# Retention and two MLPs on one core: second MLP in groups of two blocks and two chunks, first layer by seven products

## The chip, the cores and the metric

One Trainium2 chip, one core of it. The metric is the device time of one execution in microseconds (us). The engines are TensorE (PE, its weight loads are listed apart as PEld), VectorE (DVE), ScalarE (ACT), GpSimd (POOL) and SyncE (SP, whose queue SPq issues DMAs).

## What is computed

Linear attention with a decay per head, then an MLP whose activation is h·cos(h), then an MLP with a piecewise activation. There are 4·768 = 3072 tokens, a model width of 512 and a hidden width of 2048.

```python
state = gamma * state + k[t] v[t]^T ;  y[t] = scale * q[t] state      # attention, per head
h = x @ w_in;  g = h * cos(h);  x = g @ w_out                         # first MLP
h = x @ w_in                                                          # second MLP
g = where(h >= 1, h, where(h <= -1, 0, (h + 1)**2 / 4))
out = g @ w_out
```

## The kernel before

Tokens are handled in NB = 6 blocks of TB = 512, the hidden width in NF = 16 chunks of 128, the model width in NP = 4 slices of 128. Every operand of a matmul of the MLPs is kept as two tiles of type fp32r, a high part and a low part (`high_part`, an ACT copy, and `low_part`, a POOL subtraction, L100 to L108), and a product takes three matmuls: high·high, low·high and high·low. Weights arrive as 64-bit numbers and are turned into fp32 on the chip by `Convert` (L115), whose steps `one` to `six` are spread over later steps by `Conveyor` (L173).

The order of the work on each engine is written out by hand: `tc.manual_schedule()` (L637) keeps the program's order on each engine and on each DMA queue, and a tile pool makes an instruction that writes a buffer wait until those that used it have finished. A step (k, b, j) takes block b and chunk j through `first` (L396: 12 matmuls into a PSUM bank), `act` (L408: activation and the split of the result into high and low) and, LAG = 3 steps later, `second` (L463: 12 matmuls that add to four PSUM banks, which `evacuate`, L485, empties at the end of a block).

k = 0 is the first half of the first MLP's chunks, with the attention of the next block beside it, k = 1 the second half, and k = 2 the whole second MLP. During k = 1 the weights of the second MLP are converted: half of them stay in SBUF, half are stored to DRAM and come back in the first block of k = 2. In k = 2 a step is 12 matmuls of `first`, a clamp on DVE (L427), a square on ACT (L436), a maximum on DVE (L454), a copy on ACT (L455), a subtraction on DVE (L458) and 12 matmuls of `second`. The loop over k = 1 and k = 2 is L597 to L630, and L631 to L635 finish the last three steps.

## Time and profile before

| | us |
|---|---|
| median of 3 runs (lowest, highest) | 1182.93 (1182.03, 1183.85) |
| the profiled execution, its own time | 1180.83 |
| its span in the trace | 1179.0 |
| PE busy | 1150.0 (98%) |
| DVE busy | 614.6 (52%) |
| ACT busy | 522.6 (44%) |
| POOL busy | 261.8 (22%) |

The page of the profile lists the engines' busy time, the span in 40 slices, the DMA queues, the chain of work that ended last, the costliest groups of instructions and the DMA issues. A matmul is pipelined: its listed duration of 0.39 us overlaps the next one, so the rate is read from the start of one to the start of the next, or from a window's count of matmuls. DVE and ACT list overlapping durations in the same way when one instruction follows another that it doesn't depend on.

### The profile page before, as it was taken

To read this page: it belongs to the slowest core of one execution; us is meant where nothing else is said; L and a number is where in the kernel's file an instruction comes from. 1 tells how busy PE (TensorE), PEld (TensorE's weight loads), DVE (VectorE), ACT (ScalarE), POOL (GpSimd) and SP (SyncE) were. 2 spreads that over 40 slices of the span, in tenths; PEclk is the share of its full clock that TensorE was granted. 3 is DMA by queue.
4 is the path that set the end of the run, shared out by engine and by line. 5 is a ranking of instruction groups with operands and counts; after the bars stand their busy time and mean duration, and the time that the engine had idled before them with its cause. 6 is when DMAs were issued, how large, how long until landed. Compare 5 with 4: busy or idle time off the path is not lost.

```text
span 1179.0 us, 15370 instructions
## 1 busy us (share of the span) xinstructions
PE 1150.0 (98%) x6026; PEld 942.9 (80%) x6026; DVE 614.6 (52%) x981; ACT 522.6 (44%) x854; POOL 261.8 (22%) x216
## 2 busy tenths in 40 slices
PE   6788999999999999999999999999999999999998
PEld 4567888888888888888888888888888888888887
DVE  5898776565434467667765434333333433434332
ACT  3465554444436666577677423223222223223221
POOL 2665332221104212224437401001001001001000
PEclk7889999999999999999999999999999999999999
DMA  7636476453136447536425300200200200200000
GB/s 275 260 127 250 171 276 225 153 196 117 64 116 232 144 151 256 203 139 232 178 99 196 116 1 1 72 1 1 72 1 1 72 1 1 72 1 1 36 1 36
DMA packets 47848, 133.92 MB, mean 114 GB/s; under 512 B 5408, under 2 KB 5920, under 8 KB 43936
## 3 DMA queue, kind: packets, MB, share of 16 engines
q1 hardware_dynamic: 41440, 111.97, 26.9%
q10 hardware_dynamic: 6336, 20.97, 4.5%
q8 instruction: 47, 0.77, 0.3%
q14 instruction: 25, 0.20, 0.1%
HBM read 93.08 MB, written 39.85 MB: 113 GB/s over the span
## 4 chain that ended last, share of the span: by engine, by line
PE 92%; DVE 4%; DMA 1%; ACT 1%; issue 1%; SPq 0%; POOL 0%; DVEq 0%; ACTq 0%
PE b L479 44%; PE b L402 43%; PE b L284 2%; PE b L336 1%; PE b L342 1%; DVE cs L153 1%; DVE cf L138 1%; DMA raw<-in_w 1%; DMA qk<-in_qk 1%; DVE cf L149 1%; PE b L307 1%; DVE cs L134 0%; DVE pm L296 0%; DVE b L454 0%; ACT gh L455 0%
## 5 line engine op out<-in xcount | busy, mean ns | idle before, releaser
L402 PE MATMUL b<-xh,wih 128*128 128x512 f32 x768 | 302.5, 394 | 14.5 <-DVE pm L296 9.4
L402 PE MATMUL b<-xh,wil 128*128 128x512 f32 x768 | 302.7, 394 | 4.1 <-POOL wil L104 4.1
L427 DVE TENSOR_SCALAR r<-b 128x512 f32<-128x512 f32 x96 | 66.4, 691 | 304.0 <-PE b L402 304.0
L402 PE MATMUL b<-xl,wih 128*128 128x512 f32 x768 | 207.6, 393 | 0.0
L436 ACT ACTIVATE r<-r,half 128x512 f32<-128x512 f32 x96 | 69.4, 723 | 286.2 <-DVE r L427 286.2
L402 PEld LDWEIGHTS b<-xh,wih 128*128 128x128 f32 x768 | 145.8, 190 | 46.2 <-ACT wih L101 13.7
L402 PEld LDWEIGHTS b<-xh,wil 128*128 128x128 f32 x768 | 145.8, 190 | 36.3 <-POOL wil L104 6.0
L402 PEld LDWEIGHTS b<-xl,wih 128*128 128x128 f32 x768 | 146.0, 190 | 30.6
L479 PE MATMUL b<-gh,woh 128*128 128x512 f32 x384 | 153.9, 401 | 0.0
L479 PE MATMUL b<-gh,wol 128*128 128x512 f32 x384 | 149.7, 390 | 0.0
L479 PE MATMUL b<-woh,gh 128*128 128x512 f32 x384 | 149.4, 389 | 0.0
L479 PE MATMUL b<-wol,gh 128*128 128x512 f32 x384 | 149.4, 389 | 0.0
L454 DVE TENSOR_TENSOR b<-b,r 128x512 f32<-128x512 f32 x192 | 133.7, 696 | 29.7 <-ACT r L436 17.8
L159 POOL TENSOR_TENSOR cf<-cf,cs 128x512 f32<-128x512 f32 x64 | 83.0, 1297 | 294.5 <-DVE cs L153 239.6
L421 DVE SCALAR_TENSOR_TENSOR r<-b,r 128x512 f32<-128x512 f32 x96 | 66.2, 689 | 157.7 <-ACT r L416 154.6
L455 ACT ACTIVATE gh<-b 128x512 fp32r<-128x512 f32 x192 | 114.4, 596 | 74.5 <-DVE b L454 74.3
L458 DVE TENSOR_TENSOR gl<-b,gh 128x512 fp32r<-128x512 f32 x192 | 130.7, 681 | 1.8 <-ACT gh L455 0.7
L416 ACT ACTIVATE r<-b 128x512 int32<-128x512 f32 x96 | 56.9, 593 | 152.7 <-PE b L402 152.3
L104 POOL TENSOR_TENSOR xl<-xl,xh 128x512 fp32r<-128x512 f32 x24 | 30.9, 1289 | 390.7 <-ACT xh L101 390.7
L479 PE MATMUL b<-gl,woh 128*128 128x512 f32 x384 | 108.5, 389 | 0.0
L479 PE MATMUL b<-woh,gl 128*128 128x512 f32 x384 | 105.5, 389 | 0.0
L479 PEld LDWEIGHTS b<-gh,woh 128*128 128x128 f32 x384 | 72.0, 188 | 18.1 <-issue 0.7
(55 smaller groups left out, 1284.4 us busy)
## 6 DMA issues: line engine op xcount, KB each, us to landing
raw<-in_w SPq DMA_DIRECT2D x64, 512.0 KB, 5.7
qk<-in_qk SPq DMA_DIRECT2D x23, 512.0 KB, 5.4
w<-cf ACTq DMA_DIRECT2D x32, 256.0 KB, 4.3
v<-in_v SPq DMA_DIRECT2D x24, 256.0 KB, 5.5
xTh<-xh ACTq DMA_DIRECT2D x6, 1024.0 KB, 4.1
xTl<-xl ACTq DMA_DIRECT2D x6, 1024.0 KB, 6.0
yp<-o SPq DMA_DIRECT2D x24, 256.0 KB, 2.8
xh<-xTh SPq DMA_DIRECT2D x6, 1024.0 KB, 6.7
```

The costliest lines, as they stand in the source:

```text
L104: nc.gpsimd.tensor_tensor(out=lo, in0=x, in1=hi.bitcast(F32), op=ALU.subtract)
L159: nc.gpsimd.tensor_tensor(out=self.f, in0=self.f, in1=self.s.bitcast(F32), op=ALU.mult)
L284: nc.tensor.matmul(out=s2[r][:, p, :], lhsT=t[o:o + D, 1, p, :], rhs=t[o:o + D, 0, p, :], start=True, stop=True,)
L402: nc.tensor.matmul(out=h, lhsT=w[:, c * P:(c + 1) * P], rhs=x[:, c, :], start=(i == 0), stop=(i == len(terms) - 1),)
L416: nc.scalar.activation(out=n, in_=h, func=AF.Identity, scale=INV_2PI)
L421: nc.vector.scalar_tensor_tensor(out=r, in0=h, scalar=INV_2PI, in1=n, op0=ALU.mult, op1=ALU.subtract)
L427: nc.vector.tensor_scalar(out=r, in0=h, scalar1=-1.0, scalar2=1.0, op0=ALU.max, op1=ALU.min)
L436: nc.scalar.activation(out=r, in_=r, func=AF.Square, scale=0.5, bias=half)
L454: nc.vector.tensor_tensor(out=self.h, in0=self.h, in1=self.r, op=op)
L455: nc.scalar.activation(out=self.gh, in_=self.h, func=AF.Copy)
L458: nc.vector.tensor_tensor(out=self.gl, in0=self.h, in1=self.gh.bitcast(F32), op=ALU.subtract)
L479: nc.tensor.matmul(out=acc[k, b][e], lhsT=l, rhs=r, start=(begin and i == 0), stop=(last and i == 2),)
```

## The change

k = 2 is gone from the loop over steps; the class `Products` does the second MLP. It takes the six blocks in three pairs (p) and the sixteen chunks in eight pairs (l), which gives 24 groups g of two blocks and two chunks. A group's first layer is a product of 2 by 2 blocks (chunk by model half, times model half by block), done by Strassen's scheme in Winograd's form: seven products (`product`, six matmuls each, named "11", "t2", "t1", "22", "t3", "21", "t4") and sums of them on DVE (`plus`), in place in PSUM where it can be.

The sums of the weights (`combine`, four POOL operations of half width for a group) are made during k = 1 and stored to DRAM; each group loads its weights (`load_w1`, `load_w2`, from SP) and splits them (`split_w1`, `split_w2`: ACT copy, POOL subtraction). The differences of the inputs (`make`: `load`, `sub`, `parts`) are made during k = 1 for the first pair of blocks; for the other two pairs they are made while the pair before runs, up to four of the list's twenty entries at the end of each of its first five groups (`ready[:4]` in `run`), and stored to DRAM (`xb_d`) through a high-part tile `xhi` that has two buffers; `load_x` brings them back.

The clamp and the square become three ACT operations (`square`). The second layer of group g runs as eight `output`s of six matmuls between the products of group g + 1; each ends in one of PSUM banks 0 to 3, and DVE adds it to a sum in SBUF (`add`), which is stored to `out` after the eighth pair of chunks. The products use banks 4 to 7, in the order 4, 5, 6, 7, 4, 5, 4 in one group and 7, 6, 5, 4, 7, 6, 7 in the next. The high and low part of a group's last result (`late`) are made at the start of the next group.

In the loop of k = 1, conversions start in three steps of four, all results go to DRAM, `raw` has two buffers where it had three, and `cf` four where it had three.

```diff
+ORDER = ("11", "t2", "t1", "22", "t3", "21", "t4")
+LEFT = dict(zip(ORDER, ((0, 0), (1, 1), (1, 0), (2, 1), (2, 0), (0, 1), (3, 0))))
...
-        for m in range(2) for j in range(NH, NF) for a in range(2)
+        for m, j, a in [(0, j, a) for j in range(NH, NF) for a in range(2)] + [(1, j, 1) for j in range(NF)]
...
+    wa_d = [[dram.tile([P, n], F32, name=f"wa{g}{i}") for i, n in enumerate((TB, TB, TB, TB // 2))]
+            for g in range(NH)]
...
-            self.raw = self.stage.tile([P, TB, 2], I32, tag="raw", name="raw", bufs=3)
+            self.raw = self.stage.tile([P, TB, 2], I32, tag="raw", name="raw", bufs=3 - self.m)
...
-            ncs = 3 if self.m == 0 else 2
+            ncs, ncf = ((3, 3), (2, 4))[self.m]
...
-            self.f = self.stage.tile([P, TB], F32, tag="cf", name="cf", bufs=3)
+            self.f = self.stage.tile([P, TB], F32, tag="cf", name="cf", bufs=ncf)
...
+            elif (self.m, self.a) == (1, 0):
+                combine(self.j, self.f)
...
+    def combine(j, f):
+        left[j % 2] = f
+        if j % 2 == 0:
+            return
+        g, h = j // 2, TB // 2
+        a11, a12, a21, a22 = [left[i][:, o:o + h] for i in range(2) for o in (0, h)]
+        s12, s34 = [stage1[0].tile([P, TB], F32, tag=t, name=t) for t in ("s12", "s34")]
+        s1, s2, s3, s4 = [t[:, o:o + h] for t in (s12, s34) for o in (0, h)]
+        for o, x, y, op in (
+            (s1, a21, a22, ALU.add), (s3, a11, a21, ALU.subtract),
+            (s2, s1, a11, ALU.subtract), (s4, a12, s2, ALU.subtract),
+        ):
+            nc.gpsimd.tensor_tensor(out=o, in0=x, in1=y, op=op)
+        for d, t in zip(wa_d[g], (left[0], s12, s34, a22)):
+            nc.scalar.dma_start(out=d, in_=t)
...
+    class Products:
...
+        def load_w1(self, g):
+            self.w1[g] = [self.pool1("wi", NH + NP * (g % 2) + n) for n in range(NP)]
+            for d, (_, lo) in zip(wa_d[g % NH], self.w1[g]):
+                nc.sync.dma_start(out=lo[:, :d.shape[1]].bitcast(F32), in_=d)
+        def split_w1(self, g, a, b):
+            for d, (hi, lo) in list(zip(wa_d[g % NH], self.w1[g]))[a:b]:
+                split(hi[:, :d.shape[1]], lo[:, :d.shape[1]])
+        def load_w2(self, g):
+            self.w2[g] = [self.pool1("wo", NH + 2 * (g % 2) + i) for i in range(2)]
+            for i, (_, lo) in enumerate(self.w2[g]):
+                nc.sync.dma_start(out=lo.bitcast(F32), in_=w32_d[1, 2 * (g % NH) + i, 1])
+        def split_w2(self, g):
+            for w in self.w2[g]:
+                split(*w)
...
+        def make(self, p, c):
+            at, x = {}, {}
+            def load():
+                if p == 0:
+                    at.update({q: self.pool0(2 * n + c) for n, q in enumerate(ORDER)})
+                    for q in ORDER:
+                        self.x[0, q, c] = at[q]
+                    x.update({q: at[q][1].bitcast(F32) for q in ("11", "21", "22")})
+                    x["12"] = at["t4"][0].bitcast(F32)
...
+                else:
+                    for q in ORDER + ("12",):
+                        x[q] = self.tmp.tile([P, TB], F32, tag=f"x{q}", name=f"x{q}")
+                for q, j, e in (("11", 0, c), ("12", 1, c), ("21", 0, c + 2), ("22", 1, c + 2)):
+                    nc.sync.dma_start(out=x[q], in_=yT_d[2 * p + j][:, e, :])
+            def sub(o, a, b):
+                nc.gpsimd.tensor_tensor(out=x[o], in0=x[a], in1=x[b], op=ALU.subtract)
+            def parts(q):
+                if p == 0:
+                    hi, lo = at[q]
+                else:
+                    hi = self.tmp.tile([P, TB], F32R, tag="xhi", name="xhi", bufs=2)
+                    lo = x[q].bitcast(F32R)
+                high_part(hi, x[q])
+                low_part(hi, lo, x[q])
+                if p:
+                    for d, t in zip(xb_d[p, q, c], (hi, lo)):
+                        nc.sync.dma_start(out=d, in_=t.bitcast(F32))
...
+            return [
+                load,
+                some(lambda: sub("t1", "12", "11"), lambda: sub("t3", "22", "12")),
+                some(lambda: sub("t2", "22", "t1"), lambda: sub("t4", "21", "t2")),
+            ] + [lambda q=q: parts(q) for q in ORDER]
+        def load_x(self, p, n):
+            if p >= NB // 2:
+                return
+            q, c = ORDER[n // 2], n % 2
+            t = self.x[p, q, c] = self.spare.pop(0)
+            for o, d in zip(t, xb_d[p, q, c]):
+                nc.sync.dma_start(out=o.bitcast(F32), in_=d)
...
+        def product(self, g, q, i):
+            tile, half = LEFT[q]
+            p, to = g // NH, bank(i)
+            wh, wl = self.w1[g][tile]
+            xs = [self.x[p, q, c] for c in range(2)]
+            terms = [(c, w, x[0]) for c, x in enumerate(xs) for w in (wh, wl)]
+            terms += [(c, wh, x[1]) for c, x in enumerate(xs)]
+            for n, (c, w, x) in enumerate(terms):
+                o = half * 2 * P + c * P
+                nc.tensor.matmul(
+                    out=to, lhsT=w[:, o:o + P], rhs=x, start=n == 0, stop=n == len(terms) - 1
+                )
+            if g % NH == NH - 1:
+                self.free_x(p, q)
+                n = 2 * ORDER.index(q)
+                for m in range(NP + n, min(NP + n + 2, 14)):
+                    self.load_x(p + 1, m)
+            return to
+        def square(self, g, i, n, h):
+            r = tp.tile([P, TB], F32, tag="r", name="r", bufs=5)
+            nc.scalar.activation(out=r, in_=h, func=AF.Relu, scale=-0.5, bias=half)
+            nc.scalar.activation(out=r, in_=r, func=AF.Relu, scale=-1.0, bias=one)
+            nc.scalar.activation(out=r, in_=r, func=AF.Square)
+            self.g[g, i, n] = h, r
+        def high(self, g, i, n):
+            h, r = self.g[g, i, n]
+            m = self.ng % 8
+            self.ng += 1
...
-                nc.sync.dma_start(out=out[t0:t0 + P, :], in_=o)
+                gh, gl = self.pool1("wo", NF - 8 + m)
+            nc.vector.tensor_tensor(out=h, in0=h, in1=r, op=ALU.max)
+            nc.scalar.activation(out=gh, in_=h, func=AF.Copy)
+            self.g[g, i, n] = h, gh, gl
+        def low(self, g, i, n):
+            h, gh, gl = self.g[g, i, n]
+            nc.vector.tensor_tensor(out=gl, in0=h, in1=gh.bitcast(F32), op=ALU.subtract)
+            self.g[g, i, n] = gh, gl
+        def output(self, g, n, e):
+            y = bank(self.nl % 4)
+            self.nl += 1
+            s = slice(e * P, (e + 1) * P)
+            for i in range(2):
+                gh, gl = self.g[g, i, n]
+                wh, wl = self.w2[g][i]
+                for m, (a, w) in enumerate(((gh, wh), (gh, wl), (gl, wh))):
+                    nc.tensor.matmul(
+                        out=y, lhsT=a[:, s], rhs=w, start=(i, m) == (0, 0), stop=(i, m) == (1, 2)
+                    )
+            self.out.append((g, n, e, y))
+        def add(self):
+            if not self.out:
+                return
+            g, n, e, y = self.out.pop(0)
+            a = self.acc[n][:, e, :]
+            if g % NH == 0:
+                nc.vector.tensor_copy(out=a, in_=y)
+            else:
+                nc.vector.tensor_tensor(out=a, in0=y, in1=a, op=ALU.add)
+            if g % NH == NH - 1:
+                t0 = (e * NC + 2 * (g // NH) + n) * C
+                nc.sync.dma_start(out=out[t0:t0 + P, :], in_=a)
...
+        def group(self, g, outs, late):
+            more = g + 1 < self.NG
+            a, b, c, d = (4, 5, 6, 7) if g % 2 == 0 else (7, 6, 5, 4)
...
+            p1 = self.product(g, "11", a)
+            self.add()
+            for f in late[:1]:
+                f()
+            s1 = self.sums(0)
+            nc.scalar.activation(out=s1, in_=p1, func=AF.Copy)
+            for f in late[1:]:
+                f()
+            outputs(1)
+            p6 = self.product(g, "t2", b)
+            if more:
+                self.split_w1(g + 1, 0, 3)
+            self.add()
+            u = plus(self.sums(1), p6, s1)
+            outputs(1)
+            p5 = self.product(g, "t1", c)
+            self.add()
+            s5 = self.sums(2)
+            nc.scalar.activation(out=s5, in_=p5, func=AF.Copy)
+            outputs(1)
+            if more:
+                self.split_w1(g + 1, 3, NP)
+            self.split_w2(g)
+            h12 = self.product(g, "22", d)
+            self.add()
+            plus(h12, h12, u)
+            plus(h12, h12, s5)
+            self.square(g, 0, 1, h12)
+            outputs(1)
+            p7 = self.product(g, "t3", a)
+            self.add()
+            u2 = plus(self.sums(3), p7, u)
+            h22 = plus(p5, p5, u2)
+            self.high(g, 0, 1)
+            self.square(g, 1, 1, h22)
+            outputs(1)
+            self.low(g, 0, 1)
+            h11 = self.product(g, "21", b)
+            self.add()
+            plus(h11, h11, s1)
+            self.high(g, 1, 1)
+            self.square(g, 0, 0, h11)
+            outputs(1)
+            self.low(g, 1, 1)
+            h21 = self.product(g, "t4", a)
+            if g + 2 < self.NG:
+                self.load_w1(g + 2)
+            self.add()
+            plus(h21, h21, u2)
+            self.high(g, 0, 0)
+            self.square(g, 1, 0, h21)
+            outputs(1)
+            self.low(g, 0, 0)
+            self.add()
+            outputs(1)
+            if more:
+                self.load_w2(g + 1)
+            return [lambda: self.high(g, 1, 0), lambda: self.low(g, 1, 0)]
+        def run(self, before):
+            self.NG = NB // 2 * NH
+            self.tmp = sbuf("tmp", 1)
+            t = [xpool.tile([P, NP, TB], F32R, tag=t, name=t) for t in ("xh", "xl")]
+            self.spare = [[a[:, c, :] for a in t] for c in range(NP)]
+            self.load_w1(1)
+            self.load_w2(0)
+            last = parts.pop()
+            late = [last.high, last.low]
...
+            for g in range(self.NG):
+                if g == 0:
+                    outs = iter([f for b in before for f in (b, lambda: None)])
+                else:
+                    outs = iter([
+                        lambda g=g, n=n, e=e: self.output(g - 1, n, e) for n in (1, 0) for e in range(NP)
+                    ])
+                p, l = divmod(g, NH)
+                if l == 0 and p + 1 < NB // 2:
+                    ready = self.right_sides(p + 1)
+                if l == NH - 2:
+                    for n in range(NP):
+                        self.load_x(p + 1, n)
+                late = self.group(g, outs, late)
+                if g == 0:
+                    t = [xpool.tile([P, NP, TB], F32R, tag=t, name=t) for t in ("xh", "xl")]
+                    self.acc = [a.bitcast(F32) for a in t]
+                for f in ready[:4]:
+                    f()
+                ready = ready[4:]
+            for f in late:
+                f()
+            for n in (1, 0):
+                for e in range(NP):
+                    self.output(self.NG - 1, n, e)
+                    self.add()
+            while self.out:
+                self.add()
...
+            todo = [
+                Convert(1, j + i, a, False) for j in range(0, NF, 2) for a in range(2) for i in range(2)
+            ]
...
+                conv.start(todo.pop(0) if todo and k == 1 and l % 4 != 3 else None, stage)
...
+                if (k, b, l) == (1, 2, LAG + 1):
+                    ready = fast.right_sides(0)
+                if ready:
+                    fill.append(ready.pop(0))
...
+                if (k, b, l) == (1, NB - 1, NP + 1):
+                    fast.load_w1(0)
+                if (k, b, l) == (1, NB - 1, NH - 1):
+                    fast.split_w1(0, 0, NP)
...
+        fast.run([lambda i=i: evacuate(iter(second(i)), NP) for i in range(i - LAG, i)])
...
```

## Rows read from the trace of the kernel before

**Rows 1.** The page's busy time, share of the span and instructions.

```profile
PE 1150.0 (98%) x6026; PEld 942.9 (80%) x6026; DVE 614.6 (52%) x981; ACT 522.6 (44%) x854; POOL 261.8 (22%) x216
```

**Rows 2.** Windows by stage: busy (instructions) per engine, granted clock, DMA share, GB/s.

```profile
500.00:600.00 100.00, 100.00 (x442) 82.78 (x442) 70.30 (x117) 70.28 (x118) 38.46 (x29) 1.00 0.48 174
653.02:1175.21 522.19, 522.19 (x2304) 432.06 (x2302) 198.13 (x300) 145.96 (x229) 35.94 (x28) 1.00 0.07 25
```

**Rows 3.** The chain that ended last: start, length, what.

```profile
1161.62 2.72 PE b L402 x12
1164.34 10.89 PE b L479 x48
```

**Rows 4.** Groups by form, 620 to 1179 us: busy and mean ns, idle before.

```profile
L454 DVE TENSOR_TENSOR b<-b,r 128x512 f32<-128x512 f32 x102 | 71.3, 699 | 21.1 <-ACT r L436 17.8 <-ACT r L434 3.3
L427 DVE TENSOR_SCALAR r<-b 128x512 f32<-128x512 f32 x96 | 66.4, 691 | 304.0 <-PE b L402 304.0
L104 POOL TENSOR_TENSOR xl<-xl,xh 128x512 fp32r<-128x512 f32 x24 | 30.9, 1289 | 390.7 <-ACT xh L101 390.7
```

**Rows 5.** Timeline of one step, 723 to 726 us: start, length, engine, line.

```profile
723.74 0.69 DVE L427 TENSOR_SCALAR r<-b 128x512 f32<-128x512 f32 x1 [3.26 <-PE b L402]
724.34 0.68 DVE L458 TENSOR_TENSOR gl<-b,gh 128x512 fp32r<-128x512 f32 x1
724.46 0.72 ACT L436 ACTIVATE r<-r,half 128x512 f32<-128x512 f32 x1 [3.29 <-DVE r L427]
725.09 0.62 ACT L101 ACTIVATE xh<-xl 128x512 fp32r<-128x512 f32 x1
725.22 0.70 DVE L454 TENSOR_TENSOR b<-b,r 128x512 f32<-128x512 f32 x1 [0.20 <-ACT r L436]
```

**Rows 6.** DMA issues: queue, count, KB each, median us from issue to landing.

```profile
yp<-o SPq DMA_DIRECT2D x24, 256.0 KB, 2.8
yT<-o SPq DMA_DIRECT2D x24, 256.0 KB, 3.2
out<-o SPq DMA_DIRECT2D x24, 256.0 KB, 3.9
```

**Rows 7.** Timeline of a step before the second MLP, 638 to 641 us.

```profile
638.50 0.32 SPq L202 DMA_DIRECT2D wol<-w  x1
639.22 0.39 PE L402 MATMUL b<-xh,wih 128*128 128x512 f32 x1
639.34 0.62 ACT L101 ACTIVATE xh<-xl 128x512 fp32r<-128x512 f32 x1
640.04 1.30 POOL L104 TENSOR_TENSOR xl<-xl,xh 128x512 fp32r<-128x512 f32 x1 [1.59 <-ACT xh L101]
```

**Rows 8.** Windows of 1 us around two idle stretches of PE, as rows 2.

```profile
41.00:42.00 1.00, 0.00 (x0) 0.00 (x0) 1.00 (x2) 0.35 (x1) 1.00 (x1) 1.00 0.42 141
44.00:45.00 1.00, 1.00 (x4) 0.81 (x4) 0.86 (x2) 0.62 (x2) 0.76 (x2) 0.68 0.04 16
47.00:48.00 1.00, 1.00 (x9) 0.66 (x10) 0.97 (x3) 0.00 (x0) 0.00 (x0) 0.62 0.04 8
94.00:95.00 1.00, 0.00 (x0) 0.00 (x0) 1.00 (x2) 0.97 (x2) 0.00 (x0) 1.00 0.98 319
97.00:98.00 1.00, 0.64 (x3) 0.56 (x4) 1.00 (x2) 0.38 (x1) 0.30 (x1) 1.00 1.01 389
```

**Rows 9.** Timeline of PE, 43 to 57 us: matmuls after idle time.

```profile
43.02 0.50 PE L402 MATMUL b<-xh,wih 128*128 128x512 f32 x1 [2.23 <-DVE gl L458]
55.63 0.63 PE L402 MATMUL b<-xh,wih 128*128 128x512 f32 x1
56.05 0.63 PE L402 MATMUL b<-xh,wil 128*128 128x512 f32 x1
```

**Rows 10.** Timeline of DVE, 524 to 532 us: L138 without and with POOL busy.

```profile
524.62 0.42 DVE L138 TENSOR_SCALAR cf<-raw 128x512 int32<-128x512 int32 x1
531.95 1.51 DVE L138 TENSOR_SCALAR cf<-raw 128x512 int32<-128x512 int32 x1
```

More of the change, by code (lines that the diff above doesn't have):

```diff
@@ L361, in finish @@
                     nc.scalar.dma_start(out=d, in_=t.bitcast(F32))
-    JS = (range(NH), range(NH, NF), range(NF))
-    blocks = [(k, b) for k in range(3) for b in range(NB)]
+    JS = (range(NH), range(NH, NF))
+    blocks = [(k, b) for k in range(2) for b in range(NB)]
     steps = [(k, b, j) for k, b in blocks for j in JS[k]]
-    MLP = (0, 0, 1)
     hs, gs, acc, part, parts = {}, {}, {}, {}, []
@@ L396, in first @@
     def first(k, b, j, hbank):
[L397 removed]
+        (wh, wl), (xh, xl) = wt[0, j, 0], xt[k, b]
         h = bank(hbank)
@@ L432, in act @@
         evacuate(done, 2)
-        if MLP[k] == 0:
-            nc.scalar.activation(out=r, in_=r, func=AF.Sin, scale=-TWO_PI, bias=halfpi)
-        else:
-            nc.scalar.activation(out=r, in_=r, func=AF.Square, scale=0.5, bias=half)
+        nc.scalar.activation(out=r, in_=r, func=AF.Sin, scale=-TWO_PI, bias=halfpi)
         for f in mid:
```

138 lines of the change are left out of this document (72 added, 66 removed).

## The prediction

> **What bounds the kernel now.** Read the busy times first: PE 98%, the next engine 52% [rows 1]. Then the windows by stage: the second MLP lies between 653.02 and 1175.21 us, holds its 2304 matmuls (6 blocks, 16 chunks, 24 each), and PE is busy in all of its 522.19 us at the full granted clock [rows 2]. One matmul there takes 522.19 / 2304 = 0.2267 us, and the chain of waits shows the same (12 in 2.72, 48 in 10.89), without another engine in it up to the last output [rows 3]. So this stage is worth what its matmul count is worth, as long as DVE, ACT, POOL and the queues keep up.
>
> **What goes.** A pair of blocks and a pair of chunks took 2·2·12 = 48 matmuls in the first layer; it takes 7·6 = 42. The second layer keeps 2·4·6 = 48. 24 groups save 144 matmuls: 144 · 0.2267 = 32.6 us. A group is 90 matmuls, 20.40 us. The last evacuation and store stay what they are. Without any new wait the profiled execution would be 1180.8 - 32.6 = 1148.2.
>
> **What comes: the engines' sums.** DVE gets 23 operations a group (8 `add`, 7 `plus`, 4 maxima, 4 subtractions). Each takes 0.68 to 0.70 us, and independent ones start 0.60 apart (723.74, 724.34) [rows 4, 5]: 13.8 to 15.9 us of 20.4. ACT gets 24 (4 copies to `gh`, `s1` and `s5`, 6 split copies, 12 in `square`) at 0.52 to 0.72: about 15. POOL gets 5.5 split subtractions of 1.29, 7.1 us [rows 4]. None is over PE's 20.4; what matters is the order.
>
> **What comes: the chain inside a group.** Count time from the start of product "11"; products and outputs alternate, 1.36 us each. A product's result can be read 0.2 us after its slot (0.39 listed less 0.23, and 0.04 to the reader); an engine hands to another in 0.03 to 0.04 us (724.43 to 724.46) [rows 5]. Product "22" ends at 9.52, is readable at 9.72; two dependent sums on DVE end at 11.15, three ACT operations (0.70 to 0.75 each) at 13.29, the maximum at 14.46. ACT's copy `gh` then starts at 14.50. The next result's `square` is queued behind that copy: 0.50, then three operations 2.11, the maximum and its hand-overs 0.77. That is a lap of 3.38, so the copies of the four results start at 14.50, 17.88, 21.26 and 24.64, the last one at 4.2 of the next group. Its subtraction ends at 25.95, that is 5.55. The bank that it frees is written by the next group's product "22", which starts at 8.16: 2.6 us to spare. The other banks, the four outputs' banks and the split weights have 1 to 5 us. So an ordinary group costs PE nothing, which is what hides the 23 and the 24 operations; if the chain were over 2.6 us longer, every group would pay the rest.
>
> **What comes: the right sides.** After ten of the groups (0 to 4 and 8 to 12) entries of `ready` stand between a group's last `square` and the next group's `late`, on ACT. A `parts` is an ACT copy (0.62), a POOL subtraction (1.29) and two stores on SP; the third `parts` in a row writes the `xhi` that the first one's store is still reading, and ACT waits in line for that store to land. Entries fall four a group: one copy after the first group, then 4, 2, 3 and 4. No row shows such a wait; the nearest is the same shape, 256 KB from SBUF to DRAM, which lands 2.8, 3.2 or 3.9 us after its issue [rows 6]. I take 3.2, the middle one, and keep the ends. ACT's last `square` ends at 23.87; copies 1 and 2 follow at 23.77 and 24.29. Store 1 is issued at 24.4 and lands at 27.6. Store 2 stands on SP behind the low part of the first (POOL, until 25.7) and its issue of about 0.32 [rows 7], is issued at 26.1 and lands at 29.3. With four copies the last ends at 29.95, `gh` at 30.45 and the subtraction at 31.2, which is 10.8: product "22" waits 10.8 - 8.16 = 2.6 us (2.2 and 3.3 at the ends). With three copies ACT goes on after store 1: 28.25, 28.75, 29.5, which is 9.1: 0.95 us (0.55 and 1.65). With two or one nothing is late. The group after a wait starts its sums late and hands 0.2 to the next: 2.6 + 0.95 + 2.8 = 6.35 for a pair of blocks, and two pairs have it: **12.7 us (10 to 17)**. Behind ACT's wait stand `gh` and `s1`; behind `s1` stands the sum `u`, and PE gets to that later than to "22".
>
> **The clock after a wait.** Two idle stretches of PE near 2.2 us stand in the trace. After the one that ended at 43.02 the granted clock fell, 0.68 in the second after next and at the 1.2 GHz level until 47.8; after the one around 94 it stayed at 1.00 [rows 8, 9]. At the lower level matmuls start 0.42 apart (55.63, 56.05) [rows 9], so the stretch from about 44.3 to 47.8 cost 7 to 8 matmuls, 1.6 us. Of the four waits of 2.6 to 2.8 us I let two fall, as one of two rows did: **3.2 us (0 to 6.4)**.
>
> **The seams.** The first group's weights are split at the end of the last step of k = 1, behind that step's activation. In a like step [rows 7] the next product would start at 639.22, while ACT copies from 639.34 to 639.96 and POOL subtracts until 641.34: the first matmul waits 0.75, the second another 1.15, **1.9 us**. The first group has 78 matmuls (three `second` beside it, 17.7 us), so its chain, which is as long as ever, ends nearer to the next group: by the same laps "t1" waits 0.4 and "22" 0.6 there, **1.0 us**. At the end the eight outputs follow without a wait: the last pair's `gl` is ready at 25.95, and its first use of it comes after 25.84 + 1.
>
> **The second half of the first MLP.** `combine` puts four half-width POOL operations (between 0.65, half of 1.29, and 1.29 each) ahead of ACT's own stores, so ACT waits some 4 to 7 us once in four conversions; queued behind are two ACT operations of `Convert` and the next step's activation. ACT is at 70% there [rows 2], a result is used two steps (10.9 us) after it, and steps without a conversion give ACT back some 2 us. I take 0; at 1.29 each ACT would be a little over its 29 us in a cycle of 5.3 steps while the first right sides are made, and PE would lose up to 4. `raw` with two buffers makes one load in three wait for the step before; that cover is the same 10.9 us.
>
> **The sum.** -32.6 + 12.7 + 3.2 + 1.9 + 1.0 = -13.8: 1167.0 for the profiled execution. That one lies 2.1 under the median of the runs, so the forecast for the median is 1182.9 - 13.8 = **1169**.
>
> **Weighed against the Trainium skill.** In the rows a DVE clamp from PSUM takes 0.691 and an ACT operation with a bias 0.72 [rows 4, 5], so moving it to ACT as two operations lengthens each lap by one operation. The Trainium skill (ScalarE: Activation LUTs, Rules for kernel authors) has `relu`, `max` and `min` belong on VectorE; this change does the opposite. As an estimate by that page, with the clamp on DVE a lap would be some 0.7 shorter, the waits after right sides would nearly vanish, and the sum would be about 1154; the rows agree with it only on the order of the queue, not on the speed.
>
> **Rivals.** (1) *The waits are covered.* If the stores land sooner or the chain ends about 2.6 us earlier than my laps say, only the seams are left: 1182.9 - 32.6 + 2.9 = 1153. For it: each link is at most 0.05 uncertain, but 24 links add up to 1.2, and 0.95 of the three-copy wait would go first. Against: store 2 stands behind POOL's 1.29 whatever it takes itself. (2) *Slower: the chain sets every group.* Between "22" readable and the last subtraction lie about 24 links in 16.2 us. From 0.11 more a link the 2.6 are used up; from 0.16 more (3.85 in all, 1.25 over) the 29.9 us that the seams leave of the gain are gone in 24 groups; at 0.18 the 1.72 over make 1153 + 41 = 1194, at 0.25 the 3.4 over make 1235. What could do it is DVE held up while POOL works: L138 took 0.42 alone and 1.51 beside POOL [rows 10]. Against it: operations that read PSUM stay at 0.69 to 0.70 in the stage where POOL splits too [rows 4, 5], and all 23 read PSUM. The Trainium skill (SBUF — State Buffer, Who interferes with whom) says that a DVE instruction with at most one SBUF input, outside the two-port modes, does not contend with GpSimd; by that page this rival's chance would be lower still, and the trace agrees (0.70 for L454, at 725.22, next to 0.699 on average). (3) *The clock stays low longer.* All four waits and the seam fall, landing at 3.9 and 4 us of `combine`: 1182.9 - 32.6 + 17.1 + 8 + 2.9 + 4 = 1182.
>
> **How the numbers follow.** Forecast 0.50, rival 1 0.30, rival 2 0.09, rival 3 and what lies between it and the forecast 0.11. The range is 1150 (rival 1 without the seams) to 1181. Within 0.2% (2.4 us, about what a measurement of this kernel can tell from no change) lies only part of rivals 2 and 3: 0.05. Slower: the rest of rival 2, 0.08. Faster: 0.87.
>
> **What would show it.** Between the groups with right sides and the next, PE's product "22" should show a wait of 2 to 3 us that ends on a DVE subtraction, four times, and about 1 us twice; ACT, just before, a wait for a DMA of `xhi`. From group 14 on, PE should be 20.4 us a group without idle time. Matmuls should start 0.2267 apart. If ACT shows no wait for `xhi`, rival 1 holds; if every group is over 20.4, rival 2; if DVE's `plus` and `add` are over 0.75, its cause too. A wait in the second half of the first MLP would be `combine`.

## The result, and the profile after

The changed kernel is slower: 1197.74 us median (1195.95 to 1200.70) beside 1182.75 for the kernel before on the same chip, a ratio of 1.0128 [1.0106, 1.0151]. The forecast was 1169 with a range up to 1181, so both the sign and the range were wrong. The profiled execution took 1195.95, with a span of 1194.2.

The page's line of busy times after the change (busy us, share of the span, instructions), to be read beside [rows 1]:

```profile
PE 1133.1 (95%) x5882; PEld 922.3 (77%) x5882; DVE 781.3 (65%) x1233; ACT 723.0 (61%) x1212; POOL 466.9 (39%) x402
```

PE has 144 instructions fewer (6026 to 5882), as counted, and its busy time fell by 16.9 us. But its idle time, span less busy, went from 29.0 to 61.1 us. The question is where the 32.1 us of new idle time lie, so the span is cut into stages at two points of PE's chain of work: up to the last `second` beside the attention, from there to the first product of the second MLP (the last block of k = 0 and all of k = 1: the stage in which the weights of the second MLP are converted), and from there to the end of the span. The rows below the first two are the experiments, told further down.

| profiled execution | start of the last `second` beside the attention | first product | converting stage, us | second MLP, us | span |
|---|---|---|---|---|---|
| before | 337.24 | 644.66 | 307.4 | 534.3 | 1179.0 |
| after | 340.25 | 669.30 | 329.1 | 524.9 | 1194.2 |
| e1_store_later | 340.89 | 657.89 | 317.0 | 530.7 | 1188.6 |
| e2_fill_steps | 336.93 | 660.44 | 323.5 | 529.0 | 1189.4 |
| e3_no_combine | 341.62 | 656.87 | 315.3 | 525.0 | 1181.9 |
| e5_no_combine_raw3 | 340.98 | 649.25 | 308.3 | 528.1 | 1177.3 |
| e9_pairs | 341.43 | 652.25 | 310.8 | 526.4 | 1178.6 |
| e6_later_pairs | 340.95 | 649.22 | 308.3 | 525.1 | 1174.3 |
| e4_three_right_sides | 341.71 | 671.54 | 329.8 | 507.3 | 1178.8 |
| e10_early_load | 337.55 | 645.82 | 308.3 | 517.8 | 1163.6 |
| e8_all | 341.73 | 649.15 | 307.4 | 504.3 | 1153.4 |

The converting stage, which the forecast priced at 0, lost 21.7 us. The second MLP gained 9.4 of the 32.6 that its matmuls save. The stretch ahead of both is 3.0 longer, but its end moves between 336.9 and 341.7 among kernels that have the same code there, and all of the difference arises before 120 us: from 120 to 337 us PE is busy throughout at the full granted clock, before and after. In every profile with the later end the granted clock falls once more, between 97 and 105 us; in before, e2 and e10, which have the earlier end, it doesn't. One profile of each kernel stands in this table, and those of e1 and e5 took 4.6 and 4.0 us more than the medians of their kernels, so the medians further down decide what an edit was worth.

PE's waits from 384 us on, grouped by the line that waits and by what ended the wait (us in total, times, longest):

```profile
PE b L492 <- DVE o L503: 11.6, 3, 6.0
PE b L624 <- DVE gl L659: 9.8, 4, 4.7
PE b L624 <- DVE wol L659: 4.2, 3, 1.8
PE b L492 <- ACT gh L469: 2.2, 1, 2.2
PE b L671 <- DVE xh L684: 1.7, 1, 1.7
PE b L624 <- POOL wil L118: 0.8, 1, 0.8
PE b L624 <- ACT wih L115: 0.7, 1, 0.7
```

L492 is `second` of the first MLP, L624 the products, L671 the outputs. The costliest entry is a line that the prediction never spoke of: L503, the addition in `evacuate`, which empties a block's four output banks. PE's windows show what follows a long wait (window, us, PE busy and its instructions, granted clock, DMA share, GB/s):

```profile
540.00:560.00 20.00, 17.67 (x68) 0.83 0.58 198
580.00:600.00 20.00, 14.94 (x56) 0.91 0.24 89
640.00:660.00 20.00, 17.76 (x71) 0.91 0.37 125
700.00:710.00 10.00, 8.04 (x24) 0.66 0.26 99
710.00:1180.00 470.00, 460.69 (x2025) 1.00 0.42 143
1000.00:1020.00 20.00, 20.00 (x90) 1.00 0.77 279
```

How much of the lower clock fell in idle time, where it costs nothing, two more windows of PE tell; and how much a wait costs beyond its listed idle time, three lines of PE's timeline:

```profile
540.00:542.33 2.33, 0.00 (x0) 0.55 0.00 0
700.00:701.97 1.97, 0.01 (x1) 0.66 0.82 311
...
724.85 0.39 PE L671 MATMUL b<-woh,wol 128*128 128x512 f32 x1
726.99 0.50 PE L624 MATMUL b<-wih,wih 128*128 128x512 f32 x1 [1.75 <-DVE wol L659]
727.33 0.40 PE L624 MATMUL b<-wih,wil 128*128 128x512 f32 x1
```

The matmul at 724.85 is listed with 0.39 where the rate is one in 0.23, and the one behind the wait is followed after 0.34: counted by starts, a wait costs 0.16 + 0.11 = 0.27 more than is listed. So the converting stage has idle time of 6.02 + 2.20 + 2.76 + 2.82 = 13.8, another 0.7 just before the first product, and a granted clock that costs 20 · (0.17 + 0.09 + 0.09) = 7.0, of which 2.33 · 0.45 = 1.1 fell in idle time. That is 20.4 of the 21.7, and 0.27 for each of the five waits, 1.35, is about the rest. In 700 to 710 the clock costs another 3.4, of which 1.97 · 0.34 = 0.7 fell in idle time. From 710 to 1180 PE has 9.3 us of idle time, and a group without right sides (1000 to 1020, 90 matmuls) has none.

**What held the evacuation up.** The timeline after, two of the places (start, length, engine, line, operation; in brackets the idle time before it and what ended that):

```profile
534.62 1.44 POOL L204 TENSOR_TENSOR s<-cf 128x256 f32<-128x256 f32 x2
538.45 0.72 ACT L157 ACTIVATE cs<-cs,expo 128x512 int32<-128x512 int32 x1 [5.15 <-POOL s L204]
540.30 0.69 DVE L444 SCALAR_TENSOR_TENSOR r<-b,r 128x512 f32<-128x512 f32 x1 [6.31 <-ACT r L440]
541.50 1.28 DVE L503 TENSOR_TENSOR o<-b,xh 128x512 f32<-128x512 f32 x2
542.33 0.77 PE L492 MATMUL b<-gh,woh 128*128 128x512 f32 x1 [6.02 <-DVE o L503]
...
557.85 11.39 SPq L141 DMA_DIRECT2D raw<-in_w  x2
569.77 0.42 SPq L576 DMA_DIRECT2D woh<-yT  x1
575.87 1.28 POOL L579 TENSOR_TENSOR xt<-woh,wil 128x512 f32<-128x512 f32 x1 [5.61 <-DMA woh<-yT]
578.88 1.44 POOL L204 TENSOR_TENSOR s<-cf 128x256 f32<-128x256 f32 x2
581.05 1.14 ACTq L206 DMA_DIRECT2D wa<-s  x2
582.75 0.72 ACT L157 ACTIVATE cs<-cs,expo 128x512 int32<-128x512 int32 x1 [11.05 <-POOL s L204]
584.59 0.69 DVE L444 SCALAR_TENSOR_TENSOR r<-b,r 128x512 f32<-128x512 f32 x1 [9.31 <-ACT r L440]
585.10 0.50 PE L492 MATMUL b<-gh,woh 128*128 128x512 f32 x1 [2.20 <-ACT gh L469]
593.17 1.28 DVE L503 TENSOR_TENSOR o<-b,xh 128x512 f32<-128x512 f32 x2
594.00 0.47 PE L492 MATMUL b<-gh,woh 128*128 128x512 f32 x1 [2.76 <-DVE o L503]
```

Read the second place from the top. SP stands at a load of `raw` until 569.24, as `raw` has two buffers and the next one isn't free (e5 below tries a third). Queued behind that on SP are the loads that `right_sides(0)` needs, so POOL's first `sub` waits 5.61 for one. The four sums of `combine` stand behind the `sub`s on POOL. ACT issues `combine`'s four stores itself and stands at the second, the first one of a sum, from 571 to 581; behind it on ACT stand `two` of the conversion and the next activation, so DVE waits 9.31 for ACT, and PE waits for a `g` that should have been there long before. At the block's end, eight us later, DVE's addition is still late and PE waits again, 2.76. In the first place the low parts of right sides stood ahead of the sums on POOL (until 534.62), and ACT waited 5.15.

At that end there is the least cover of the whole stage. This is read from the program. The four output banks are evacuated in the step whose `second` was the block's last, and `second` of the next block writes them one step, 24 matmuls or 5.4 us, later. In mid-block a late result has two steps.

**In the second MLP**, the timeline after shows three kinds of wait:

```profile
695.05 2.13 SPq L576 DMA_DIRECT2D x<-yT  x4
700.07 0.63 ACT L115 ACTIVATE xhi<-x 128x512 fp32r<-128x512 f32 x1 [4.60 <-DMA x<-yT]
701.97 0.79 PE L624 MATMUL b<-wih,wih 128*128 128x512 f32 x1 [4.68 <-DVE gl L659]
...
714.37 0.60 ACT L654 ACTIVATE woh<-b 128x512 fp32r<-128x512 f32 x1 [0.77 <-DVE b L653]
717.73 0.60 ACT L654 ACTIVATE woh<-b 128x512 fp32r<-128x512 f32 x1 [0.77 <-DVE b L653]
722.98 0.63 ACT L115 ACTIVATE xhi<-x 128x512 fp32r<-128x512 f32 x1 [1.60 <-DMA xb1t20h<-xhi]
725.09 0.63 ACT L115 ACTIVATE xhi<-xt 128x512 fp32r<-128x512 f32 x1 [1.48 <-DMA xb1t10h<-xhi]
...
1182.54 0.68 DVE L684 TENSOR_TENSOR xh<-b,xh 128x512 f32<-128x512 f32 x1
1183.27 0.50 PE L671 MATMUL b<-woh,woh 128*128 128x512 f32 x1 [1.71 <-DVE xh L684]
```

First, after the first group ACT waits 4.60 for a load of x that SP could issue only at 695.05, behind four loads of `load_w1` and two of `load_w2`; PE then waits 4.68 and runs at the lower clock for some 6 us. Second, ACT's waits for the stores of `xhi`, in the very place that the prediction named, and behind them PE's wait of 1.75 at product "22" (726.99, above). Third, 1.71 at the very end. The budget: 534.3 - 32.6 = 501.7 would be the stage without a new wait; it took 524.9, that is 23.2 more. The seam 0.85 (its other part, 0.69, lies before the first product and so in the converting stage); first group 4.68 + 2.7 for the clock = 7.4, the same wait after the ninth group (at 873.68) 1.5; waits after right sides 1.75 + 1.75 + 1.71 + 0.74 + 1.86 = 7.8; the end 1.7. That is 19.3. Nine waits cost about 0.27 each beyond what is listed, 2.4; and 1.1 are eight matmuls that start 0.07 to 0.28 late with no wait listed, four of them in the second group. That leaves 0.4.

### The profile page after: what moved, and what is told of

It reads as the page before. It is cut to its first block, busy times and chain, and to the rows that moved or that the text cites. A ratio compares the mean times of both kernels' runs of the same rounds, so it can differ in the third digit from the quotient of the medians.

```text
span 1194.2 us, 16523 instructions
## 1 busy us (share of the span) xinstructions
PE 1133.1 (95%) x5882; PEld 922.3 (77%) x5882; DVE 781.3 (65%) x1233; ACT 723.0 (61%) x1212; POOL 466.9 (39%) x402
## 4 chain that ended last, share of the span: by engine, by line
PE 56%; DVE 12%; DMA 11%; ACT 8%; issue 7%; POOL 4%; SPq 1%; ACTq 0%; DVEq 0%; POOLq 0%
PE b L671 16%; PE b L624 14%; PE b L492 11%; PE b L427 10%; DMA raw<-in_w 6%; DVE cs L167 2%; DVE cf L152 2%; PE b L319 2%; DVE cf L163 2%; PE b L371 1%; ACT r L639 1%; DVE cs L148 1%; POOL s L204 1%; DVE b L653 1%; PE b L377 1%
## 5 line engine op out<-in xcount | busy, mean ns | idle before, releaser
L118 POOL TENSOR_TENSOR wil<-wil,wih 128x512 fp32r<-128x512 f32 x108 | 123.6, 1176 | 244.1 <-ACT wih L115 204.4
L492 PE MATMUL b<-gh,woh 128*128 128x512 f32 x384 | 156.4, 407 | 13.8 <-DVE o L503 11.6
L427 PE MATMUL b<-xh,wih 128*128 128x512 f32 x384 | 153.9, 401 | 15.0 <-DVE pm L331 9.3
L427 PE MATMUL b<-xh,wil 128*128 128x512 f32 x384 | 154.2, 402 | 2.9 <-POOL wil L118 2.9
L492 PE MATMUL b<-gh,wol 128*128 128x512 f32 x384 | 152.3, 397 | 0.0
L492 PE MATMUL b<-gl,woh 128*128 128x512 f32 x384 | 110.2, 394 | 0.1
L427 PE MATMUL b<-xl,wih 128*128 128x512 f32 x384 | 106.2, 400 | 0.0
L492 PEld LDWEIGHTS b<-gh,woh 128*128 128x128 f32 x384 | 73.1, 190 | 33.6 <-ACT o L507 12.8
L427 PEld LDWEIGHTS b<-xh,wih 128*128 128x128 f32 x384 | 74.1, 193 | 31.5 <-ACT wih L115 14.0
L706 DVE TENSOR_TENSOR b<-b,sum 128x512 f32<-128x512 f32 x120 | 83.4, 695 | 18.7 <-PE b L624 15.3
L492 PEld LDWEIGHTS b<-gl,woh 128*128 128x128 f32 x384 | 73.6, 192 | 16.1 <-DVE gl L472 0.5
L492 PEld LDWEIGHTS b<-gh,wol 128*128 128x128 f32 x384 | 73.4, 191 | 14.2
L624 PE MATMUL b<-wih,wih 128*128 128x512 f32 x176 | 70.0, 398 | 14.8 <-DVE gl L659 9.8
L118 POOL TENSOR_TENSOR wol<-wol,woh 128x512 fp32r<-128x512 f32 x58 | 74.7, 1309 | 20.6 <-ACT woh L115 18.8
L671 PE MATMUL b<-woh,woh 128*128 128x512 f32 x192 | 74.9, 390 | 1.7 <-DVE xh L684 1.7
```

Of the source, the lines that this page charges most:

```text
L118: nc.gpsimd.tensor_tensor(out=lo, in0=x, in1=hi.bitcast(F32), op=ALU.subtract)
L427: nc.tensor.matmul(out=h, lhsT=w[:, c * P:(c + 1) * P], rhs=x[:, c, :], start=(i == 0), stop=(i == len(terms) - 1),)
L492: nc.tensor.matmul(out=acc[k, b][e], lhsT=w[:, s], rhs=g, start=(begin and i == 0), stop=(last and i == 2),)
L624: nc.tensor.matmul(out=to, lhsT=w[:, o:o + P], rhs=x, start=n == 0, stop=n == len(terms) - 1)
L671: nc.tensor.matmul(out=y, lhsT=a[:, s], rhs=w, start=(i, m) == (0, 0), stop=(i, m) == (1, 2))
L706: nc.vector.tensor_tensor(out=o, in0=x, in1=y, op=ALU.add)
```

## The experiments

The letters are those of the expectations. Theory A: in the converting stage ACT, standing at the stores of `combine`, makes the evacuation late, and PE pays at block ends. Rival B: the additional work itself is too much where the right sides lie beside an evacuation. Rival C: `raw` has two buffers, and DVE waits for its loads. For the second MLP the theory is the `xhi` ring and the late first load. Ratios are to the kernel before on the same chip, with a 95% interval, and "worth" is the difference from after's 1.0128, times 1183 us; by the intervals it is uncertain by some 3 us.

| kernel | median, us | ratio | worth, us |
|---|---|---|---|
| e1_store_later | 1185.78 | 1.0019 [1.0001, 1.0037] | 12.9 |
| e2_fill_steps | 1191.19 | 1.0076 [1.0049, 1.0104] | 6.2 |
| e3_no_combine | 1184.26 | 1.0008 [0.9988, 1.0029] | 14.2 |
| e5_no_combine_raw3 | 1175.07 | 0.9938 [0.9916, 0.9959] | 22.5 |
| e9_pairs | 1178.90 | 0.9959 [0.9945, 0.9973] | 20.0 |
| e6_later_pairs | 1175.75 | 0.9934 [0.9917, 0.9951] | 23.0 |
| e4_three_right_sides | 1179.47 | 0.9965 [0.9954, 0.9977] | 19.3 |
| e10_early_load | 1166.62 | 0.9864 [0.9848, 0.9881] | 31.2 |
| e8_all | 1154.88 | 0.9758 [0.9743, 0.9772] | 43.8 |

**e1: `combine`'s stores a step later.** Sums, stores and their number stay; only the place on ACT's queue changes.

```diff
-        for d, t in zip(wa_d[g], (left[0], s12, s34, a22)):
-            nc.scalar.dma_start(out=d, in_=t)
+        stores.append(list(zip(wa_d[g], (left[0], s12, s34, a22))))
...
         def advance(self):
+            if stores:
+                for d, t in stores.pop(0):
+                    nc.scalar.dma_start(out=d, in_=t)
```

> The stores of combine are issued one step later, so that ScalarE doesn't stand before them while GpSimd still makes the sums; the work is the same. Theory A (ScalarE's waits for combine, 5.2 and 11.1 us among them, make the block ends late in the second half of the first MLP): its waits there fall from 19.2 us to under 6, TensorE's idle stretches of 6.0, 2.2, 2.8 and 2.8 us go, and the time is 1197.7 - 17 = 1181 (1177 to 1186). Theory B (the work itself is too much where the right sides lie beside the end of a block): at most one of the four stretches goes, 1190 to 1196. Theory C (raw has two buffers, VectorE waits 18.4 us for its loads): no change, 1195 to 1199.

ACT's waits for POOL's sums, 19.2 us after the change, are gone, and the converting stage is 12.1 us shorter. PE's waits at its block ends, and DVE's waits for `raw` in the stage, in e1:

```profile
PE b L494 <- DVE o L505: 5.8, 1, 5.8
DVE cs L148 <- DMA raw<-in_w: 32.6, 16, 4.6
```

Three of four waits of PE are gone, one of 5.8 is left, again on the evacuation. So the stores' place is a cause, and not the only one: DVE still waits 32.6 us for `raw` (30.6 in the stage after the change, 14.8 before it).

**e2: no right sides in the steps next to an evacuation.**

```diff
-                if ready:
+                if ready and l not in (1, 2):
```

> The right sides of the first pair are left out of steps 1 and 2 of a block and come later; nothing else moves. Theory B: the stretches of 6.0, 2.8 and 2.8 us, all just after a block's sums are evacuated in step 2, go: 1197.7 - 15 = 1183. Theory A: ScalarE still waits for combine behind other right sides; half of it goes, 1187 to 1195. Theory C: 1195 to 1199.

PE's three waits at block ends stay (3.9, 1.3 and 4.1). They are shorter than after's 6.02, 2.76 and 2.82 in sum, by what goes with ACT's shorter wait for POOL (14.7 instead of 19.2): right sides are part of what POOL is late by, and moving them was worth 6.2, where B had expected some 15: their falling into these steps does not set the waits.

**e3: no sums at all.**

```diff
-        for o, x, y, op in (
-            (s1, a21, a22, ALU.add), (s3, a11, a21, ALU.subtract),
-            (s2, s1, a11, ALU.subtract), (s4, a12, s2, ALU.subtract),
-        ):
-            nc.gpsimd.tensor_tensor(out=o, in0=x, in1=y, op=op)
-        for d, t in zip(wa_d[g], (left[0], s12, s34, a22)):
+        for d, t in zip(wa_d[g], (left[0], left[1], left[0], a22)):
```

> Leaves out the sums of combine and stores the converted weights in their place (so the second MLP multiplies other weights). It prices combine: no GpSimd work and no wait of ScalarE. Theories A and B: the four idle stretches go, 1197.7 - 18 = 1180 (1177 to 1185), within 3 us of the run with later stores if it is the wait (A), and some 8 us under it if it is the work (B). Theory C: VectorE's waits for raw stay, 1192 to 1199.

Without the sums the second MLP multiplies other weights; the count and order of its operations stay. The time is that of e1 within the intervals, 1.4 us apart, though POOL has 32 operations less, where B had expected some 8 us. So with the stores later it is not POOL's work on the sums that costs, but who waits for it. C alone, at 1192 or more, does not fit either, yet it isn't gone: PE's waits of 0.9 and 4.1 on the evacuation are left, and DVE waits 38.7 us for `raw`, more than the 30.6 of after.

**e5: e3 with the third buffer of `raw`.** The third buffer takes the room of the sums, so this stands on e3, and the same edit on the full change was not tried.

```diff
-            self.raw = self.stage.tile([P, TB, 2], I32, tag="raw", name="raw", bufs=3 - self.m)
+            self.raw = self.stage.tile([P, TB, 2], I32, tag="raw", name="raw", bufs=3)
```

> As the run without combine (1184.3; the sums of the weights are left out, so the second MLP multiplies other weights), with three buffers for raw as before the change; the room comes from the sums. Theory (with combine's waits gone, the idle 5 us of TensorE that are left at block ends come from VectorE waiting 38.7 us for raw): those waits fall to some 10 us, the idle stretches of 0.9 and 4.1 us and the half clock after them go, 1184.3 - 7 = 1177 (1175 to 1180). Rival (the right sides beside the evacuation are what is left): unchanged, 1182 to 1187.

DVE's waits for `raw` in the converting stage of e5:

```profile
DVE cs L148 <- DMA raw<-in_w: 1.3, 1, 1.3
```

38.7 became 1.3, PE has no wait left before the second MLP but the seam's 0.69, and the stage takes 308.3 beside 307.4 before the change. The second cause is the ring of `raw`, C: three starts in a row with two buffers.

**e9: other steps for the conversions.** On the changed kernel alone: two starts and a pause, from four steps before k = 1 on, in place of three starts and a pause from k = 1 on.

```diff
-                conv.start(todo.pop(0) if todo and k == 1 and l % 4 != 3 else None, stage)
+                pos = i - len(steps) + NB * NH + NP
+                conv.start(todo.pop(0) if todo and pos >= 0 and pos % 3 != 2 else None, stage)
```

> Conversions start in two of three steps, from the middle of the last block of the first half on, instead of in three of four; raw keeps two buffers, and no load has to wait for the step before. Combine's stores stay where they are. Theory (raw and combine each cost, about 8 and 12 of the 21 us): VectorE's waits for raw fall under 12 us, ScalarE's for combine stay at 15 to 20 us, the time is 1197.7 - 8 = 1190 (1186 to 1193). Rival (all of it is combine): 1196 to 1199.

The waits in the converting stage of e9:

```profile
ACT cs L157 <- POOL s L204: 19.9, 4, 5.9
DVE cs L148 <- DMA raw<-in_w: 17.8, 5, 5.5
PE b L492 <- DVE o L505: 1.2, 1, 1.2
PE b L492 <- DVE o L503: 0.8, 1, 0.8
```

This was worth far more than expected. ACT stands at the stores as long as before (19.9), only its longest wait fell from 11.0 to 5.9; DVE's waits for `raw` fell from 30.6 to 17.8, and PE waits 2.0 in place of 13.8. The two causes do not add up (12.9 and 20.0 alone, 23.0 together in e6). I read it so: each eats of the same 5.4 us of cover at a block's end, and PE pays only for what is over. The timeline above gives a second reason: loads of `raw` stood ahead of the right sides' loads on SP, and these ahead of the sums, so freeing `raw` can shorten ACT's longest wait as well. No run parts the two. The expected time was too high because it gave each cause a share of PE's waits to itself.

**e6: e1 and e9 together.**

> Both: combine's stores one step later, and conversions in two of three steps. Theory (the two together are the whole loss of the second half of the first MLP): TensorE has no idle stretch before the second MLP, and the time is 1197.7 - 21 = 1177 (1175 to 1180). Rival (the right sides and the sums of the weights are too much work for ScalarE and GpSimd): an idle stretch of 3 to 6 us at a block end stays, 1182 to 1188.

No wait of PE before the second MLP but the seam's 0.69, 308.3 for the stage, with the same sums and the same right sides on the same engines: so the work as such, B, is not too much for the stage. From here on only the second MLP is left.

**e4: right sides three a group, the first load before the first group.** On the changed kernel, so its converting stage is as bad as ever (329.8).

```diff
                 if l == 0 and p + 1 < NB // 2:
                     ready = self.right_sides(p + 1)
+                    ready.pop(0)()
...
-                for f in ready[:4]:
+                for f in ready[:3]:
                     f()
-                ready = ready[4:]
+                ready = ready[3:]
```

> In the second MLP three entries of the right sides after a group instead of four, and each list's first loads before its first group. Theory (the third and fourth part in a row wait for a store of xhi, the first for its load): the waits of product 22 of 4.7, 1.75, 1.75, 1.5, 1.7, 0.7 and 1.9 us go, and the half clock after the first: 1197.7 - 16 = 1182 (1180 to 1187). Rival (ScalarE has too much in these groups whatever the order): the same total of some 14 us, spread over seven groups instead of five, 1195 to 1199.

One of eight like waits of ACT, and what is left of PE's waits at the products, in e4:

```profile
ACT xhi L115 <- DMA xb1t30h<-xhi: 1.6, 1, 1.6
PE b L624 <- DVE gl L659: 0.3, 1, 0.3
```

The time is a little below the expected range. ACT still waits 1.6 to 1.8 for a store, eight times, but only one copy after a group waits instead of two, and PE doesn't notice. The second MLP is 17.6 shorter; waits after right sides, first group and its clock, and the ninth group were 7.8 + 7.4 + 1.5 = 16.7 of the budget above, and 0.27 more for each of seven waits makes 18.6.

**e10: e6 with the early load alone, still four a group.**

> As the run with combine's stores later and conversions in pairs (1175.8), with the first loads of each list of right sides issued before its first group; four entries a group stay (so 2, 4, 1, 4 and 3 parts a group). It prices the two waits of the second MLP apart. Theory: the wait of 4.8 us after the first group, the half clock behind it (some 3.4 us lost) and the 1.3 us after the ninth group go, and the waits of 1.7 to 2 us after groups with four parts stay, four of them: 1175.8 - 10 = 1166 (1164 to 1169). Rival (the first wait is the first group's shortness, not the load): 1174 to 1177.

Measured as expected: 8.3 us from e6 for the load alone (first group's wait 4.79 in e6, 0.50 here, and none after the ninth group). The four-copy waits are there as before, 1.89, 1.39, 1.71 and 2.17, which parts the two causes that e4 took away together.

**e8: all of it**, that is e6 and e4, the first group's weights split in two steps, and the last group's high and low part queued between the additions of the end.

```diff
-            for f in late:
-                f()
             for n in (1, 0):
                 for e in range(NP):
                     self.output(self.NG - 1, n, e)
                     self.add()
+                    if n == 1 and 0 < e < 3:
+                        late.pop(0)()
...
+                if (k, b, l) == (1, NB - 1, NH - 2):
+                    fast.split_w1(0, 0, 2)
                 if (k, b, l) == (1, NB - 1, NH - 1):
-                    fast.split_w1(0, 0, NP)
+                    fast.split_w1(0, 2, NP)
```

> Both of these, three entries of right sides a group with the first loads early, the first two weight tiles of the second MLP split one step earlier, and in the tail the last result's parts made between the adds. Theory: everything that the change added on TensorE's path goes, and 144 matmuls are saved: 1183 - 32.6 + 1 = 1151 (1149 to 1156). Rival (something that no wait shows is left in the second MLP, some 3 us there): 1156 to 1162.

e8: the page's busy times, PE's only wait after 384 us, and PE's window from 700 to 1140 us:

```profile
PE 1121.1 (97%) x5882; PEld 916.4 (79%) x5882; DVE 782.8 (68%) x1233; ACT 723.7 (63%) x1212; POOL 468.3 (41%) x402
PE b L626 <- DVE gl L661: 0.3, 1, 0.3
700.00:1140.00 440.00, 439.88 (x1940) 1.00 0.42 146
```

1154.88, 2.4% below the kernel before and 3.6% below the changed one, with the same 5882 matmuls and the same sums. The converting stage is back at 307.4, and the second MLP takes 504.3, 30.0 less than before, of the 32.6 that were counted. Of the other 2.6, 2.2 are, by starts, thirteen matmuls that begin 0.07 to 0.51 late, six of them in the second group (1.3 in sum).

## Why the prediction was wrong, and where it was right

**The step that failed: "The second half of the first MLP … I take 0".** It cost 21.7 us in the profiled execution. The prediction had both mechanisms in hand, ACT behind `combine` and `raw`'s ring, named a wait there as `combine`'s sign, and let both vanish in a cover of "two steps (10.9 us)". Three things were wrong in that one step.
- The cover. It holds in mid-block, while at each block's end the evacuation leaves one step, 5.4 us; PE's waits of 6.02, 2.76 and 2.82 all end on L503. The page and the chain of before showed no wait there, since nothing was late then.
- ACT's wait. "4 to 7" was 5.2 in one place and 11.05 in another, because POOL's queue, too, had a wait ahead of the sums: `sub`s whose loads stood on SP behind `raw`. The prediction costed the four sums (it had 0.65 to 1.29 for one; in these two places they took 0.72 to 0.74), but not what they stood behind, and for `raw` it did not name what else is queued on SP.
- The addition. Each delay was held against the whole cover by itself. e1, e9 and e6 show that the two act together (12.9 and 20.0 alone, 23.0 for both), and e5 that without both the stage takes what it took before, within 1 us. That they spend one cover is a reading that fits; no run shows it apart from the second reason given at e9.

The profiled span grew by 15.2 where a fall of 13.8 was forecast, 29.0 apart: 21.7 are this step, which alone turns 1169 into 1190.7, 4.4 the second MLP (23.2 less 18.8), and 3.0 lie ahead of the converting stage. "Up to 4" was no bound, and the 4 us that rival 3 gave to `combine` neither: they counted ACT's load and not its waits in line.

**The terms of the second MLP** gave 18.8 to the bad; 23.2 were measured. That the sum is near is in part luck: the right sides were 4.9 too high and the first group 6.4 too low.
- *The saving*: 32.6 counted; e8 shows 30.0 of it in the second MLP. Right.
- *The chain inside a group*: a lap of 3.38 foretold, 3.36 measured (714.37 to 717.73), and groups without right sides run without idle time, 20.40 from one to the next. Right; so rival 2 didn't happen, and "slower" came by a mechanism that was no rival.
- *Right sides*: the place, the order and the four-copy cases are as foretold; of the two three-copy cases, about 1 each foretold, one had 0.74 and one none. The size was too high: the stores of `xhi` landed 2.3 us after their issue in the median of 28 (2.0 to 4.3; behind the second group 2.0 to 2.4), not 3.2 [rows 6], and PE waited 1.75, not 2.6. Put into the prediction's own working, 2.1 for the landing gives 2.6 - 1.1 = 1.5. In all 7.8, or 9.2 by starts, under the range's 10 either way. The nearest row was not that near: before the change the `out` stores of a block's end are issued 0.4 to 0.6 us apart, and in the first four blocks the first of four landed after 2.4 to 2.5 and the others after 3.9 to 4.3. e4 and e10 show the mechanism.
- *The clock*: two falls for 3.2 foretold. In the profile after there is none after waits of 1.5 to 1.9, and one with the first group's wait, 2.7 of it in PE's busy time. But this differs from profile to profile: with the same second MLP e1 has two falls and e2 three, after waits of 1.82 to 1.92, so the forecast's two of four lie within what was seen.
- *The seams*: 1.5 for the first, 1.9 foretold; right. The first group: 1.0 foretold, 4.68 and 2.7 for the clock measured. The prediction listed `load` as one of the entries of `ready` and costed the copies and stores of `parts`, but not the wait of the first `parts` for that load, nor what SP had ahead of it (e10: 8.3 for issuing the first load of each list before its group instead of behind it).
- *The end*: 0 foretold, 1.7 measured. The prediction looked at when `gl` is ready, not at `late`'s place on DVE ahead of the additions that empty the banks; e8, which moves it, has no wait there.

DVE's operations that read PSUM kept their 0.68 to 0.70 beside POOL's work, as the prediction had it, though its own row could hardly show that: L454 at 725.22 [rows 5] shares only its last 0.13 us with POOL's subtraction at 725.79. After the change it can be shown. An add of `plus` under a stretch of POOL, and the group that most of these belong to, from 669 to 1194 us (count, busy and mean ns, idle before):

```profile
727.29 4.50 POOL L118 TENSOR_TENSOR wil<-wil,wih 128x512 fp32r<-128x512 f32 x4 [0.22 <-ACT wih L115]
727.45 0.68 DVE L706 TENSOR_TENSOR sum<-b,sum 128x512 f32<-128x512 f32 x1
L706 DVE TENSOR_TENSOR b<-b,sum 128x512 f32<-128x512 f32 x120 | 83.4, 695 | 18.7 <-PE b L624 15.3
```

Of the operations of L706, 91 lie by more than four fifths beside an operation of POOL and take 0.693 in the mean, 63 lie beside none and take 0.692.

**Open**: why the granted clock fell once more at about 100 us in eight of the eleven profiles; the small late starts in the second group of the second MLP; and whether the two causes of the converting stage share a cover or stand one behind the other.

## What to carry to other kernels

When work is moved into an earlier stage, price it where that stage has its *shortest* cover (here the block ends, one step instead of two), and don't give each delay that cover to itself. A DMA issue on a compute engine's queue is a wait of that engine for whatever produces the data: follow it back through each queue, here ACT to POOL to SP to a ring of two buffers, and put it where its data is surely done. A load that is issued where it is needed starts behind everything that its queue was given before.

## What the runs showed of the hardware

- No length of idle time parts the waits of PE that the granted clock followed with a fall to 0.50 (the 1.2 GHz level) from those that it didn't. In after it fell beside the waits of 2.76, 2.82, 4.68 and 6.02 us, for 3.4 to 6.8 us, and stayed at 1.00 after 2.20 (585.10) and after six waits of 1.5 to 1.9. In e2 it fell after 1.83, 1.86 and 1.92, and in e4 it stayed at 1.00 after 3.03. PE's windows behind the wait of 1.92 in e2 and of 3.03 in e4:

```profile
865.60:872.00 6.40, 6.36 (x21) 0.73 0.13 50
587.40:596.00 8.60, 6.02 (x24) 1.00 0.32 123
```

- The same store of 256 KB from SBUF to DRAM (`out`) landed after 2.0 us in the median after the change, where such stores are issued 0.6 us or more apart, and after 3.9 before it, where most are issued 0.4 to 0.6 apart. `yp` landed after 2.9, and `yT`, with the conversions beside it, after 5.3 (2.8 and 3.2 before the change [rows 6]).
